# Rows of minus the row maxima in an attention kernel: split on VectorE as columns and turned by an ordinary product, in place of a transpose that is split after it

## The chip, the cores and the metric

The kernel runs on one core of a Trainium2 chip. The metric is the device time of one execution in microseconds (us); smaller is better. The time before is the median of three runs.

## The reference, cut to what matters

One transformer block with adaptive layer norm: softmax attention with 32 heads of width 16 over 2048 tokens of width 512, then a dense layer, Mish, and a dense layer (width 1792). What the change touches is the softmax:

```python
scores = jnp.einsum("bhqd,bhkd->bhqk", q, k) * scale
p = _softmax(scores, axis=-1)
o = jnp.einsum("bhqk,bhkd->bhqd", p, v)
```

A softmax subtracts from each row of scores (one query, one head) the largest score of that row before the exponential.

## The kernel before, in words

**Rounds and steps.** The work is cut into `NIT` = 32 rounds, one for each block of 512 queries and each group of four heads. A round has 16 steps; there are 512 steps after a prologue of `PRO` = 20. In every step TensorE makes, for the present round, four score products (L531, 128 keys by 512 queries, 64 rows of contraction each) that ScalarE turns into exponentials (L534), and the four products with V of two steps earlier (`pv`, L549). The maxima have to be known before the round begins, so in the same step TensorE also makes four products of a round that is one or two ahead (L482, 128 queries by 512 keys), of which VectorE takes the maxima (L484). The projections, the MLP and everything else are cut into pieces that stand beside these eight products (L135, on the other half of TensorE's rows). `step` writes the order of each engine by hand; an engine takes its instructions in that order.

**The ring.** The results of L482 and L531, and some others, go to `ring`, six banks of PSUM that are handed out in turn (`NRING` = 6). The ring gives a bank again after six others, so a product waits until the reader of the result six places earlier is done. In a step the order is maximum, score, maximum, score, maximum, score, score, maximum; below these are called m1 s1 m2 s2 m3 s3 s4 m4. So s4 waits for VectorE's reduction of m1 of the same step, and m4 for ScalarE's exponential of s1 of the same step.

**How the maxima get into the scores.** [...] The maxima come out of VectorE as columns (128 queries on the partitions), and are needed as rows.

**The functions that the change touches.** `neg_max(n)` is called at the end of the last maximum step of round n, t % 16 = 11 counted by steps, after that step's products. It reduces the four partial maxima of each query (`mx`, 128 x 64 values) to 16 values, twice (L505, v = 0 and 1), so that `mm` holds each maximum two times, 128 x 32. One step later, at the end of step t % 16 = 12 after `pv`, `max_rows(n, mm)` runs: TensorE transposes `mm` (L511) into a bank of the ring (32 x 128); ScalarE makes minus that, rounded to the short format, `mh` (L513); VectorE makes `mt` (L514): with the column `lows`, which is 0 for the high rows and -1 for the low rows, `mt` is `mh * lows - pt`, so minus the maximum in the high rows and the rounding's remainder in the low rows. In the step after that SyncE issues four DMAs (L520) that put `mt` into `qa`, where the scores of round n read it three steps later.

**Queues.** VectorE's queue in these steps holds the four reductions of each step and, between them, `neg_max` and the third instruction of `max_rows`; at some steps also a part of Mish (L732) or a reciprocal (L584). ScalarE's holds the exponentials, L513 and parts of Mish (L741 among them). GpSimd (POOL) does long element-wise work on 128 x 512 tiles in SBUF all along (L735 to L753, L95, L98, L820, L899).

Of the kernel before, what the change touches and what calls it, by code (L numbers as in the profile page):

```python
# [8 lines left out]
F32 = mybir.dt.float32  # L9
F32R = mybir.dt.float32r  # L10
AF = mybir.ActivationFunctionType
ALU = mybir.AluOpType
AX = mybir.AxisListType
# [5 lines left out]
def adaln_block(ctx: ExitStack, tc: tile.TileContext, x, wqkv, wo, w1, b1, w2, c, w_mod, out):  # L19
    nc = tc.nc  # L20
    P = 128
# [25 lines left out]
    out = out[0]  # L47
# [3 lines left out]
    cst = ctx.enter_context(tc.tile_pool(name="cst", bufs=1))  # L51
# [11 lines left out]
    ident = cst.tile([P, P], F32, name="ident")  # L63
# [10 lines left out]
    nc.gpsimd.memset(sel, 0.0)  # L74
    for k in range(DK):
        nc.gpsimd.memset(sel[32 * k:32 * k + 1, :], 1.0)
    lows = cst.tile([P, 1], F32, name="lows")
    nc.vector.tensor_reduce(out=lows[:32], in_=ident[:32, :32].rearrange("p (a v q) -> p v a q", a=4, v=2)[:, 1], op=ALU.add,
                            axis=AX.XY)
    nc.vector.tensor_scalar_mul(lows[:32], lows[:32], -1.0)  # L80
    modc = cst.tile([P, 4, DK], F32, name="modc")
    sil = cst.tile([P, DK], F32, name="sil")
    b1c = cst.tile([P, FT], F32, name="b1c")
# [66 lines left out]
    def ring(w=1):  # L150
        if w == 2 and ring_at[0] % 2:
            ring_at[0] += 1
        b = ring_at[0] % NRING
        ring_at[0] += w
        return ring_t[:, b, :] if w == 1 else ring_t[:, b:b + 2, :]
# [41 lines left out]
    def at(h, f):  # L197

        hooks.setdefault(h, []).append(f)
# [121 lines left out]
    with ExitStack() as es:  # L321
# [68 lines left out]
        for i in range(2):  # L390
            pr.append(ring())
            for k in range(DK):
                nc.tensor.matmul(pr[i][32 * k:32 * k + 32, :], sil[:, k:k + 1].to_broadcast([P, 32]), wma[i][:, k, :],
                                 start=True, stop=True)
# [68 lines left out]
    ap = ctx.enter_context(tc.tile_pool(name="ap", bufs=1, reuse_waits="tile"))  # L463
# [36 lines left out]
    def neg_max(n):  # L500

        mx = mxs.pop(n)
        mm = ap.tile([P, 4, 2, 4], F32, tag="mm", name="mm", bufs=2)
        for v in range(2):
            nc.vector.tensor_reduce(out=mm[:, :, v, :], in_=mx.rearrange("p s (j q) k -> p (s j) q k", j=2), op=ALU.max,  # L505
                                    axis=AX.X)
        ats.setdefault(16 * n + 16 - PRO, []).append(lambda: max_rows(n, mm))

    def max_rows(n, mm):
        pt = ring()  # L510
        nc.tensor.transpose(pt[:32, :P], mm.rearrange("p a v q -> p (a v q)"), ident)  # L511
        mh, mt = [ap.tile([32, P], F32R, tag=t, name=t, bufs=1) for t in ("mh", "mt")]
        nc.scalar.activation(mh, pt[:32, :P], AF.Identity, scale=-1.0)  # L513
        nc.vector.scalar_tensor_tensor(mt, mh.bitcast(F32), lows[:32], pt[:32, :P], op0=ALU.mult, op1=ALU.subtract)  # L514

        def put():
            for s in (1, 0):
                for j in range(2):
                    o = (2 * s + j) * 8
                    nc.sync.dma_start(  # L520
                        qa[(2 * n + j) % NR][64 * s + 48:64 * s + 50, :].rearrange("v (s q) -> v s q", s=4).bitcast(F32),
                        mt[o:o + 8, :].bitcast(F32))
        at(2 * (16 * n + 16 - PRO) + 2, put)
# [649 lines left out]
    def step(t):  # L1173
# [4 lines left out]
        if t < 0:  # L1178

            for i in range(2):  # L1180
                if tm < 16:
                    kb, jq = divmod(2 * tm + i, 8)
                else:
                    jq, kb = tm % 16 // 2, 2 * second + i
                max_pair(tm // 16, jq, kb)
            if second and tm % 16 == 15:
                neg_max(tm // 16)
            run_hooks(2 * t + 1)
            for f in ats.pop(t, []):
                f()  # L1190
            whole_units(2 * t + 1, CREDIT)
            do_specials(2 * t + 1)
            return
# [58 lines left out]
        if tm < T and tm % 16 == 15:  # L1252
            neg_max(tm // 16)
# [111 lines left out]
    t = T + 2  # L1365
# [32 lines left out]
```

## Time and profile before

| what | value |
|---|---|
| runs | 1705.08, 1706.13, 1705.99 us; median 1705.99 |
| span of the profiled execution | 1705.4 us; the page gives no time of that execution apart from its span |
| granted TensorE clock | 0.998 of full speed, mean over the span |
| busy: PE, PEld, DVE, ACT, POOL | 1678.7, 956.8, 1439.9, 1364.9, 808.0 us |
| L482, products for maxima | 1968, mean 427 ns |
| L484, their reductions | 1968, mean 682 ns |
| L534, exponentials | 2048, mean 601 ns |
| DMA | 240.08 MB, mean 141 GB/s |

How to read it: busy time counts overlapping instructions of one engine once; the end of a matmul is modelled, so a busy PE does not tell that TensorE could do no more. PEld is TensorE's loading of the stationary operand; its start is the better sign of when TensorE really turned to a product. An entry `[0.84 <-DVE mx L484]` in a timeline means that the engine stood idle 0.84 us and that the last semaphore it had waited for came from that instruction, which may have been given long before.

### The profile page before, as it was taken

The page shows a single profiled execution, that of the slowest core. Times are in us where ns is not written, and L with a number is a line of the kernel's source. Part 1 is how long each engine was busy: PE and PEld are TensorE (multiplying, and loading weights), DVE is VectorE, ACT ScalarE, POOL GpSimd, SP SyncE. Part 2 cuts the span into 40 slices and gives each one's busy share as a digit, 9 for nine tenths or more (in the row PEclk, how much of TensorE's full clock was granted, in tenths as well). Part 3 has the DMA queues.
Part 4 walks back from the last instruction along what each step waited for, and adds up shares of the span by engine and source line. Part 5 has one row for each costly group of instructions (what it writes and reads, how often), then busy time and mean ns, then how long its engine had stood idle before and what let it go on. Part 6 is the DMA issues. An engine that isn't in the chain of part 4 may idle for free.

```text
span 1705.4 us, 33628 instructions
## 1 busy us (share of the span) xinstructions
PE 1678.7 (98%) x12372; PEld 956.8 (56%) x12372; DVE 1439.9 (84%) x2368; ACT 1364.9 (80%) x2613; POOL 808.0 (47%) x829
## 2 busy tenths in 40 slices
PE   7999999999999999999999999999999999999999
PEld 5755655555445555555555555555555455554587
DVE  6888888888889998888889998888889988883377
ACT  6257777777778988888888988888888988888574
POOL 5155224665413464655423564555323655555442
PEclk9999999999999999999999999999999999999999
DMA  7677467777773342534355433424354433524261
GB/s 253 183 235 210 116 161 213 242 228 221 237 209 100 98 105 78 137 79 123 84 154 145 119 75 94 139 74 125 85 144 124 128 93 78 150 59 156 85 228 63
DMA packets 113997, 240.08 MB, mean 141 GB/s; under 512 B 24048, under 2 KB 49648, under 8 KB 107784
## 3 DMA queue, kind: packets, MB, share of 16 engines
q1 hardware_dynamic: 113832, 237.92, 48.8%
q8 instruction: 98, 1.61, 0.4%
q14 instruction: 67, 0.55, 0.1%
HBM read 179.95 MB, written 51.44 MB: 136 GB/s over the span
## 4 chain that ended last, share of the span: by engine, by line
PE 90%; DMA 4%; DVE 3%; ACT 1%; SPq 1%; issue 1%; POOL 0%; ACTq 0%; DVEq 0%; POOLq 0%
PE bk L549 28%; PE ring L482 21%; PE ring L531 19%; PE bk L135 12%; PE bk L129 3%; PE ring L1110 2%; PE ring L129 2%; DVE mx L484 1%; DMA qa<-mt 1%; DMA ka<-kscr 1%; DMA xt<-in_A_x 1%; PE ring L496 1%; ACT pr L534 1%; DMA w<-woscr 1%; DMA w<-w1scr 0%
## 5 line engine op out<-in xcount | busy, mean ns | idle before, releaser
L484 DVE TENSOR_REDUCE mx<-ring 128x1 f32<-128x512 f32 x1968 | 1222.1, 682 | 157.7 <-PE ring L482 134.1
L534 ACT ACTIVATE pr<-ring 128x512 f32<-128x512 f32 x2048 | 1085.6, 601 | 215.5 <-PE bk L135 131.2
L482 PE MATMUL ring<-ka,qa 64*128 64x512 f32 x1968 | 834.2, 427 | 5.2 <-DMA od<-ot 2.7
L531 PE MATMUL ring<-qa,ka 64*128 64x512 f32 x2048 | 724.5, 397 | 4.2 <-ACT pr L534 2.2
L482 PEld LDWEIGHTS ring<-ka,qa 64*128 64x128 f32 x1968 | 359.6, 184 | 405.8 <-DVE mx L484 341.2
L549 PE MATMUL bk<-pr,vg 128*32 128x512 f32 x4096 | 545.1, 604 | 0.0
L531 PEld LDWEIGHTS ring<-qa,ka 64*128 64x128 f32 x2048 | 373.8, 184 | 81.3 <-ACT pr L534 23.6
L135 PE MATMUL bk<-h,w 64*128 64x512 f32 (+1 forms) x1080 | 280.2, 393 | 0.1
L135 PE MATMUL bk<-w,a_h 64*128 64x512 f32 x632 | 213.0, 417 | 0.3 <-ACT pr L534 0.2
L135 PEld LDWEIGHTS bk<-h,w 64*128 64x128 f32 x1080 | 178.2, 184 | 12.3 <-ACT pr L534 3.7
L549 PEld LDWEIGHTS bk<-pr,vg 128*32 128x32 f32 x4096 | 80.7, 108 | 132.0 <-issue 124.6
L135 PE MATMUL bk<-w,a_l 64*128 64x512 f32 x316 | 124.0, 392 | 0.0
L135 PEld LDWEIGHTS bk<-w,a_h 64*128 64x128 f32 x632 | 104.7, 184 | 16.6 <-ACT pr L534 8.3
L899 POOL TENSOR_TENSOR y<-yd,y 128x512 f32<-128x512 f32 x44 | 56.8, 1292 | 89.5 <-ACT yd L898 84.4
L750 POOL TENSOR_TENSOR qq<-qq,rr 128x512 f32<-128x512 f32 x42 | 54.3, 1292 | 89.8 <-ACT rr L744 89.6
L734 POOL TENSOR_SCALAR qq<-ee 128x512 f32<-128x512 f32 x25 | 15.5, 619 | 168.0 <-ACT ee L728 168.0
L736 POOL TENSOR_TENSOR hb<-hb,ee 128x512 f32<-128x512 f32 x42 | 54.1, 1288 | 82.5 <-DVE ee L732 80.5
L135 PE MATMUL bk<-w,o_hl 64*128 64x512 f32 x288 | 79.6, 408 | 0.0
L98 POOL TENSOR_TENSOR a_l<-hb,a_h 128x512 fp32r<-128x512 f32 x53 | 72.0, 1359 | 4.4
L135 PEld LDWEIGHTS bk<-w,a_l 64*128 64x128 f32 x316 | 58.3, 184 | 3.9
L135 PE MATMUL bk<-h_h,wl 64*128 64x512 f32 x168 | 56.7, 418 | 0.0
L752 POOL TENSOR_TENSOR rr<-rr,qq 128x512 f32<-128x512 f32 x42 | 54.2, 1291 | 3.5
(189 smaller groups left out, 1844.2 us busy)
## 6 DMA issues: line engine op xcount, KB each, us to landing
ka<-kscr SPq DMA_DIRECT2D x124, 384.0 KB
w<-w2scr SPq DMA_DIRECT2D x56, 512.0 KB
w<-w1scr SPq DMA_DIRECT2D x46, 512.0 KB
vg<-vscr SPq DMA_DIRECT2D x32, 552.0 KB
qa<-qscr SPq DMA_DIRECT2D x124, 100.0 KB
kscr<-qh SPq DMA_DIRECT2D x16, 512.0 KB
qscr<-qh SPq DMA_DIRECT2D x32, 256.0 KB
hl<-in_B_w SPq DMA_DIRECT2D x28, 256.0 KB
```

The lines of the kernel that those rows point to most:

```text
L98: (nc.gpsimd if eng == "p" else nc.vector).tensor_sub(lo, src, hi.bitcast(F32))
L129: nc.tensor.matmul(acc, l, r, start=start, stop=stop)
L135: i = nc.tensor.matmul(acc, l[64 * g:64 * g + 64], r[64 * g:64 * g + 64], start=start and not g, stop=bool(stop and g))
L482: nc.tensor.matmul(pm, qt[64 * s:64 * s + 64, qs * P:(qs + 1) * P], kt[64 * s:64 * s + 64, kb * TB:(kb + 1) * TB], start=True, stop=True)
L484: nc.vector.tensor_reduce(out=mxs[n][:, s, 4 * j + qs, kb:kb + 1], in_=pm, op=ALU.max, axis=AX.X)
L531: nc.tensor.matmul(p_, kt[64 * s:64 * s + 64, kc * P:(kc + 1) * P], qt[64 * s:64 * s + 64, :], start=True, stop=True)
L534: e = nc.scalar.activation(pr, p_, AF.Exp, scale=SCALE)
L549: nc.tensor.matmul(accs[n][32 * h:32 * h + 32, :], vgs[n][:, o:o + 32], pts.pop((t, h)), start=(kc == 0), stop=(kc == 15))
L736: (nc.vector if tail else nc.gpsimd).tensor_mul(hb, hb, ee)
L750: nc.gpsimd.tensor_mul(qq, qq, rr)
L752: nc.gpsimd.tensor_mul(rr, rr, qq)
L899: nc.gpsimd.tensor_add(y[i], yd, y[i])
```

## The change

Minus the maximum and its split are made as columns, before the turn, and the turn is an ordinary product with an identity matrix that is kept in the short format. `neg_max` takes one reduction to a new tile `top` (one buffer), a multiplication by -1 that writes the high part rounded to the short format, and a `scalar_tensor_tensor` that takes the high part from minus `top` for the low part. `max_rows` multiplies `mm` with `identr`, and ScalarE copies the result to `mt`. `lows`, `mh` and VectorE's instruction on `mt` go. The DMAs, the steps in which things are issued and the ring's use stay.

```diff
-    lows = cst.tile([P, 1], F32, name="lows")
-    nc.vector.tensor_reduce(out=lows[:32], in_=ident[:32, :32].rearrange("p (a v q) -> p v a q", a=4, v=2)[:, 1], op=ALU.add,
-                            axis=AX.XY)
-    nc.vector.tensor_scalar_mul(lows[:32], lows[:32], -1.0)
+    identr = cst.tile([P, P], F32R, name="identr")
+    nc.vector.tensor_copy(identr, ident)
...
         mx = mxs.pop(n)
-        mm = ap.tile([P, 4, 2, 4], F32, tag="mm", name="mm", bufs=2)
-        for v in range(2):
-            nc.vector.tensor_reduce(out=mm[:, :, v, :], in_=mx.rearrange("p s (j q) k -> p (s j) q k", j=2), op=ALU.max,
-                                    axis=AX.X)
+        top = ap.tile([P, 4, 4], F32, tag="top", name="top", bufs=1)
+        mm = ap.tile([P, 4, 2, 4], F32R, tag="mm", name="mm", bufs=2)
+        nc.vector.tensor_reduce(out=top, in_=mx.rearrange("p s (j q) k -> p (s j) q k", j=2), op=ALU.max, axis=AX.X)
+        nc.vector.tensor_scalar_mul(mm[:, :, 0, :], top, -1.0)
+        nc.vector.scalar_tensor_tensor(mm[:, :, 1, :], top, -1.0, mm[:, :, 0, :].bitcast(F32), op0=ALU.mult,
+                                       op1=ALU.subtract)
         ats.setdefault(16 * n + 16 - PRO, []).append(lambda: max_rows(n, mm))
 
     def max_rows(n, mm):
         pt = ring()
-        nc.tensor.transpose(pt[:32, :P], mm.rearrange("p a v q -> p (a v q)"), ident)
-        mh, mt = [ap.tile([32, P], F32R, tag=t, name=t, bufs=1) for t in ("mh", "mt")]
-        nc.scalar.activation(mh, pt[:32, :P], AF.Identity, scale=-1.0)
-        nc.vector.scalar_tensor_tensor(mt, mh.bitcast(F32), lows[:32], pt[:32, :P], op0=ALU.mult, op1=ALU.subtract)
+        nc.tensor.matmul(pt[:32, :P], mm.rearrange("p a v q -> p (a v q)"), identr, start=True, stop=True)
+        mt = ap.tile([32, P], F32R, tag="mt", name="mt", bufs=1)
+        nc.scalar.copy(mt, pt[:32, :P])
```

## The prediction, made before the changed kernel was run

> **What bounds the kernel now.** I read the page first, then the timelines of two neighbouring steps, engine by engine.
>
> ```profile
> span 1705.4 us, 33628 instructions
> PE 1678.7 (98%) x12372; PEld 956.8 (56%) x12372; DVE 1439.9 (84%) x2368; ACT 1364.9 (80%) x2613; POOL 808.0 (47%) x829
> ```
>
> TensorE is nearly always busy, VectorE and ScalarE not far behind. Which of them ends a step is seen in the loads of TensorE's stationary operands. Below, one step with the transpose (661.03 to 664.18) and the next without (664.18 to 667.02):
>
> ```profile
> 661.03 0.16 PEld L549 LDWEIGHTS bk<-pr,vg 128*32 128x32 f32 x8 [0.25 <-issue]
> 662.03 0.10 PEld L511 LDWEIGHTS ring<-ident,mm 128*32 128x32 f32 x1 [0.84 <-DVE mx L484]
> 662.24 0.18 PEld L482 LDWEIGHTS ring<-ka,qa 64*128 64x128 f32 x1
> ...
> 663.64 0.18 PEld L531 LDWEIGHTS ring<-qa,ka 64*128 64x128 f32 x1 [0.17 <-DVE mx L484]
> 663.76 0.18 PEld L482 LDWEIGHTS ring<-ka,qa 64*128 64x128 f32 x1
> 664.18 0.16 PEld L549 LDWEIGHTS bk<-pr,vg 128*32 128x32 f32 x8 [0.24 <-issue]
> 665.18 0.18 PEld L482 LDWEIGHTS ring<-ka,qa 64*128 64x128 f32 x1 [0.84 <-DVE mx L484]
> ...
> 666.46 0.18 PEld L531 LDWEIGHTS ring<-qa,ka 64*128 64x128 f32 x1
> 666.60 0.18 PEld L482 LDWEIGHTS ring<-ka,qa 64*128 64x128 f32 x1
> 667.02 0.16 PEld L549 LDWEIGHTS bk<-pr,vg 128*32 128x32 f32 x8 [0.25 <-issue]
> ```
>
> The plain step lasts 667.02 - 664.18 = 2.84 us, the one with the transpose 3.15. The 0.84 us of idle time ahead of the first L482 are the products with V still running, not VectorE. Of the 0.31 us more, 662.24 - 662.03 = 0.21 are the transpose itself; the other 0.10 arise at the step's end.
>
> ```profile
> 659.38 0.35 DVE L505 TENSOR_REDUCE mm<-mx 128x16 f32<-128x64 f32 x2
> 659.71 2.48 DVE L484 TENSOR_REDUCE mx<-ring 128x1 f32<-128x512 f32 x4
> 662.65 0.33 DVE L514 SCALAR_TENSOR_TENSOR mt<-mh,lows,ring 32x128 fp32r<-32x128 f32 x1 [0.45 <-ACT mh L513]
> 662.91 2.47 DVE L484 TENSOR_REDUCE mx<-ring 128x1 f32<-128x512 f32 x4
> 665.71 2.48 DVE L484 TENSOR_REDUCE mx<-ring 128x1 f32<-128x512 f32 x4 [0.33 <-PE ring L482]
> ```
>
> VectorE's four reductions take 2.48 of the 2.84 us; it then idles about 0.35 us. But it is not free: the ring ties s4 to the reduction of m1. In the plain step that reduction starts at 665.71, 0.53 after the product's load, and lasts about 0.69 (to 666.40); s4's load follows at 666.46. A later start of the first reduction moves that load. The slack is read from the step with the transpose: there the first reduction starts at 662.91, 0.67 after the product's load instead of 0.53, s4's load follows it by 1.40 instead of 1.28, and yet the matmul keeps its pace:
>
> ```profile
> 663.51 0.40 PE L531 MATMUL ring<-qa,ka 64*128 64x512 f32 x1
> ...
> 663.74 0.39 PE L531 MATMUL ring<-qa,ka 64*128 64x512 f32 x1
> ```
>
> 0.23 us apart, about the pace of other products. So VectorE may be some 0.12 us late at the start of a step; what is over comes out of TensorE's time and is lost. The step's path is TensorE's, with VectorE and ScalarE tied within a tenth of a microsecond.
>
> **The change part by part.** It acts in 31 rounds (that of the first lies in the prologue).
>
> ```profile
> L505 DVE TENSOR_REDUCE mm<-mx 128x16 f32<-128x64 f32 x64 | 11.1, 215 | 1.1
> L514 DVE SCALAR_TENSOR_TENSOR mt<-mh,lows,ring 32x128 fp32r<-32x128 f32 x32 | 10.7, 333 | 15.9 <-ACT mh L513 15.9
> L511 PE MATMUL ring<-ident,mm 128*32 128x128 f32 x32 | 9.1, 284 | 0.0
> L513 ACT ACTIVATE mh<-ring 32x128 fp32r<-32x128 f32 x32 | 8.5, 266 | 11.0 <-PE ring L511 11.0
> L1110 PE MATMUL ring<-w,a_h 128*128 128x512 f32 x112 | 34.9, 393 | 0.0
> L129 PE MATMUL bk<-wl,h_h 128*128 128x256 f32 x48 | 8.2, 287 | 0.0
> ```
>
> *The turn.* Products in the short format take 393 ns for 512 columns and 287 ns for 256, so 106 ns for 256 columns; by that line 128 columns take 287 - 53 = 234, against 284 for the transpose: 0.05 us less in each round, -1.6 us in 31. No row has such a product with 128 columns. It can hardly take longer than one with 512 (393): +0.11 a round, +3.4 us. I take the line. [...]
>
> *VectorE's instruction on `mt` and its wait.* 0.33 us busy and 15.9 / 32 = 0.50 idle go in each round. In the step above this buys nothing: it made the first reduction 0.14 late, about the slack. What is late next is m4, which waits for s1's exponential. I count 0, at most the 0.10 at the step's end: -3.1 us.
>
> *ScalarE* keeps one small instruction (266 ns; the copy is of the same size). It takes over the waits for the last DMAs out of `mt`, while it idles 11.0 / 32 = 0.34 us for the turn anyway: 0. If that cover went, the exponentials behind it would be late by what is waited for. *The DMAs* into `qa` go out about 0.4 us earlier (no 0.33, no wait for `mh`), SyncE's queue frees as much earlier; no DMA is added. TensorE's matmuls waited for them 1.2 us in all:
>
> ```profile
> L531 PE MATMUL ring<-qa,ka 64*128 64x512 f32 x2048 | 724.5, 397 | 4.2 <-ACT pr L534 2.2 <-DMA qa<-mt 1.2 <-DVE mx L484 0.4
> ```
>
> 0 to -1.2 us; I take 0. The constants at the start are one small instruction instead of two, hidden by the first loads.
>
> *VectorE's columns.* The pair of reductions runs overlapped, 0.35 us from 659.38, and the next reduction followed at 659.71 without a gap: the pair just fills the idle time. Now there are three instructions, each reading what the one before wrote.
>
> ```profile
> 3.22 0.19 DVE L352 TENSOR_SCALAR sil_e<-sil_e 128x4 f32<-128x4 f32 x1 [1.57 <-ACT sil_e L351]
> 3.44 0.18 DVE L353 RECIPROCAL sil_e<-sil_e 128x4 f32<-128x4 f32 x1
> 3.66 0.16 DVE L354 TENSOR_TENSOR sil<-cc,sil_e 128x4 f32<-128x4 f32 x1
> ```
>
> Such a chain costs 0.16 to 0.19 each and 0.03 to 0.04 between (3.22 + 0.19 to 3.44). So 0.215 + 0.035 + 0.16 + 0.035 + 0.18 = 0.63 us instead of 0.35: the next reduction starts up to 0.28 later. 0.12 of that is slack, so between 0 (where the idle time is longer) and 0.16 us a round are lost. I take the middle, as no row says how the idle times lie: 31 x 0.08 = +2.5 us, bounds 0 and +5.0. `mm` is needed a step later, so its own lateness is hidden.
>
> *GpSimd in the way.* The last of the three, a `scalar_tensor_tensor`, reads two tensors in SBUF; the instruction on `mt` read one there and one in PSUM. An instruction with two SBUF inputs that meets a running GpSimd instruction is seen here:
>
> ```profile
> 599.37 1.74 DVE L732 SCALAR_TENSOR_TENSOR ee<-ee 128x512 f32<-128x512 f32 x1
> 601.04 3.07 DVE L484 TENSOR_REDUCE mx<-ring 128x1 f32<-128x512 f32 x5
> ```
> ```profile
> 599.27 1.29 POOL L753 TENSOR_TENSOR hb<-hb,rr 128x512 f32<-128x512 f32 x1
> ```
> ```profile
> L747 DVE SCALAR_TENSOR_TENSOR rr<-qq,rr 128x512 f32<-128x512 f32 x14 | 9.7, 692 | 0.5
> ```
> ```profile
> 599.80 0.16 PEld L549 LDWEIGHTS bk<-pr,vg 128*32 128x32 f32 x8 [0.24 <-issue]
> ...
> 602.96 0.18 PEld L531 LDWEIGHTS ring<-qa,ka 64*128 64x128 f32 x1 [0.41 <-DVE mx L484]
> ...
> 603.39 0.16 PEld L549 LDWEIGHTS bk<-pr,vg 128*32 128x32 f32 x8 [0.24 <-issue]
> ```
>
> It takes 1.74 us where 0.69 is usual: it ends 0.55, the time of its 512 elements, after GpSimd's instruction ends (599.27 + 1.29 = 600.56). TensorE's step there lasts 3.59 us instead of 2.84; s4's load waits for VectorE. So the wait is real and is paid. How often does GpSimd run where the new instruction will stand? I took the 31 stretches from 0.44 to 0.64 us after the first L505 (columns: length, then busy time of PE, PEld, DVE, ACT, POOL); the first, the last and the sum:
>
> ```profile
> 138.84:139.04 0.20, 0.20 (x4) 0.20 (x2) 0.20 (x1) 0.04 (x1) 0.12 (x2) 1.00 0.54 221
> ...
> 1548.21:1548.41 0.20, 0.20 (x6) 0.16 (x3) 0.00 (x0) 0.20 (x1) 0.20 (x1) 1.00 0.00 0
> sum 6.19, PE 5.97 PEld 5.25 DVE 5.59 ACT 2.17 POOL 3.50; mean PE 0.19 PEld 0.17 DVE 0.18 ACT 0.07 POOL 0.11
> ```
>
> GpSimd is busy in 3.50 of 6.19, 57%: some 17 of 31. With 1.29 us a GpSimd instruction, the mean rest is 0.64; less the slack and what the instruction would have taken, about 0.45. But only 13 rows show POOL busy for the whole 0.20; in two of them VectorE has no reduction waiting, and I leave out three more for instructions that end soon after. 8 x 0.45 = +3.6 us. Bounds: 0 (a 16-element instruction slips through) and 17 x 0.64 = +10.9.
>
> *Sum:* -1.6 + 0 + 0 + 2.5 + 3.6 = +4.5 us on the span of 1705.4, that is 1709.9. The span lies 0.6 below the median of the runs, 1705.99, so the forecast is 1710.5.
>
> **The rivals.** *The multiplication waits for GpSimd too.* It reads one SBUF tensor; no row shows such an instruction beside a running GpSimd. If it waits, it runs when GpSimd's instruction ends, and the `scalar_tensor_tensor` behind it meets the next GpSimd instruction, 0.09 us later (L753 ended 600.56; the next one is recorded at 600.65):
>
> ```profile
> 600.65 0.94 POOL L95 TENSOR_SCALAR a_h<-hb 128x512 fp32r<-128x512 f32 x1
> ```
>
> Each of the 8 places then costs 0.2 more, or, where the second wait is lost as well, about 1.3 more: 1712 to 1721; I set 1716. [...]
>
> *The chain hides and GpSimd does not matter:* -1.6 + 2.5 = +0.9, 1706.9.
>
> *VectorE's freed 0.83 us is what the step with the turn lacks.* The place is its end: if all 0.10 us come from the first reduction's 0.14 delay behind `mt`, they go in 31 rounds, -3.1; with the turn -4.7; and the chain must cost less than the 0.12 slack: 1701.3. For it: the wait of 0.17 us for VectorE ahead of the load at 663.64. Against: the matmul after it was on time, and the late one, m4 at 663.76, waits for ScalarE. It decides from the point where the longer chain stays within 0.12 us.
>
> [...]
>
> **How the numbers follow.** Forecast 1710.5: 0.42, its own range 1707 to 1714. Both wait: 0.20. Hidden: 0.18. Freed: 0.12. Slow product: 0.08. About 0.2%, 3.4 us, is what a measurement of this kernel can tell from no change. Faster by more (below 1702.6) is the freed case: 0.12. Within: the hidden one and 0.07 of the forecast's low end: 0.25. Slower (above 1709.4): 0.35 + 0.20 + 0.08 = 0.63. The range 1703 to 1721 leaves out most of the freed case and little above.
>
> **What would show it.** The load of L482 follows the turn's load by 0.16 us (0.21 now); by 0.3 if the product is slow. VectorE's `scalar_tensor_tensor` on `mm` has a median near 0.2 us and a maximum near 1 us; if its median too is long, or the multiplication's maximum is, the first rival holds. The steps that begin after `neg_max` grow (2.84 to 2.9, or 3.3 beside GpSimd); no VectorE idle time before `mt`. I am wrong if these steps stay at 2.84, or if the step with the turn falls from 3.15 by much more than 0.05.

## The result, and the profile after

| kernel | median of the runs, us | runs |
|---|---|---|
| before | 1706.06 | 6, 1705.08 to 1711.08 |
| after | 1718.14 | 6, 1715.0 to 1722.61 |

The ratio is 1.0063, with a 95% interval of 1.0044 to 1.0082: the changed kernel is slower, by some 10.7 us (0.0063 x 1706; 7.5 to 14.0 by the interval). The forecast was slower, 1710.5, a growth of 4.5 us. Direction and range held the result; the size was less than half of it.

The profiled execution took 1721.08 us with this span, 2.9 us over the median. The page:

```profile
span 1719.2 us, 33649 instructions
PE 1687.5 (98%) x12372; PEld 960.6 (56%) x12372; DVE 1444.8 (84%) x2367; ACT 1365.4 (79%) x2613; POOL 808.3 (47%) x829
```

VectorE's share of the span has not moved, 84%. The share cannot show what happened, because an instruction that waits inside the engine counts as busy: L504 below has 385 ns of busy time on average, up to 975, where its shortest takes 174. The same round as in the prediction, TensorE's loads of stationary operands in the step after `neg_max` (662.14 to 665.14) and in the step with the turn (665.14 to 668.25); L480 is the product for a maximum, L530 the score product, L548 the product with V. Before, the step after `neg_max` ran from 658.19 to the 661.03 that the prediction shows, 2.84 us; its first line, then the lines after:

```profile
658.19 0.16 PEld L549 LDWEIGHTS bk<-pr,vg 128*32 128x32 f32 x8 [0.25 <-issue]
```
```profile
662.14 0.16 PEld L548 LDWEIGHTS bk<-pr,vg 128*32 128x32 f32 x8 [0.24 <-issue]
663.13 0.18 PEld L480 LDWEIGHTS ring<-ka,qa 64*128 64x128 f32 x1 [0.84 <-DVE mx L482]
...
664.65 0.18 PEld L530 LDWEIGHTS ring<-qa,ka 64*128 64x128 f32 x1 [0.29 <-DVE mx L482]
664.72 0.18 PEld L480 LDWEIGHTS ring<-ka,qa 64*128 64x128 f32 x1
665.14 0.16 PEld L548 LDWEIGHTS bk<-pr,vg 128*32 128x32 f32 x8 [0.24 <-issue]
666.14 0.11 PEld L511 LDWEIGHTS ring<-identr,mm 128*32 128x32 f32 x1 [0.84 <-DVE mx L482]
666.32 0.18 PEld L480 LDWEIGHTS ring<-ka,qa 64*128 64x128 f32 x1
...
668.25 0.16 PEld L548 LDWEIGHTS bk<-pr,vg 128*32 128x32 f32 x8 [0.24 <-issue]
```

And VectorE in the same steps:

```profile
663.36 0.22 DVE L503 TENSOR_REDUCE top<-mx 128x16 f32<-128x64 f32 x1
663.61 0.17 DVE L504 TENSOR_SCALAR mm<-top 128x16 fp32r<-128x16 f32 x1
663.82 0.18 DVE L505 SCALAR_TENSOR_TENSOR mm<-top,mm 128x16 fp32r<-128x16 f32 x1
663.91 2.48 DVE L482 TENSOR_REDUCE mx<-ring 128x1 f32<-128x512 f32 x4
666.85 2.48 DVE L482 TENSOR_REDUCE mx<-ring 128x1 f32<-128x512 f32 x4 [0.46 <-PE bk L133]
```

In this round no GpSimd instruction holds the three up (one begins at 663.82, together with the third, which takes its usual 0.18). The step after `neg_max` lasts 3.00 us. Its first reduction starts 0.78 us after its product's load (663.91 - 663.13) and no longer 0.53. The last score product (s4) waits 0.29 us for it: the load of s4 is 1.52 us behind that of m1, where it was 1.28. The step with the turn lasts 3.11 us and not 3.15, although its first reduction is no longer late (666.85 is 0.53 after 666.32).

The small groups (columns: busy time, mean ns of one, idle time before and what ended it; `fp32r` is the short format, `F32R` in the code):

```profile
L504 DVE TENSOR_SCALAR mm<-top 128x16 fp32r<-128x16 f32 x32 | 12.3, 385 | 1.1
L513 ACT CAST mt<-ring 32x128 fp32r<-32x128 f32 x32 | 8.1, 254 | 15.9 <-PE ring L511 15.9
L511 PE MATMUL ring<-identr,mm 128*32 128x128 f32 x32 | 8.0, 249 | 0.3 <-DVE mm L505 0.3
L503 DVE TENSOR_REDUCE top<-mx 128x16 f32<-128x64 f32 x32 | 7.0, 220 | 1.1
L505 DVE SCALAR_TENSOR_TENSOR mm<-top,mm 128x16 fp32r<-128x16 f32 x32 | 6.6, 207 | 1.1
```

The same two VectorE lines with minimum, median and maximum of one instruction in ns:

```profile
L504 DVE TENSOR_SCALAR mm<-top x32: 174/210/975, 93.8 to 1560.9; 128x16 fp32r<-128x16 f32 x32
L505 DVE SCALAR_TENSOR_TENSOR mm<-top,mm x32: 174/176/1189, 94.1 to 1561.7; 128x16 fp32r<-128x16 f32 x32
```

The prediction expected the long durations on L505, the instruction with two inputs in SBUF. They are on L504, the multiplication, which has one: mean 385 ns, up to 975. It took 243 ns or more in 16 of its 32 rounds, and by GpSimd's timeline these are exactly the 16 in which a GpSimd instruction was running when it started; in the others it took 174 to 177. Round 17, VectorE and then GpSimd, whose only instruction in these 7 us this is:

```profile
895.27 0.22 DVE L503 TENSOR_REDUCE top<-mx 128x16 f32<-128x64 f32 x1
895.52 0.97 DVE L504 TENSOR_SCALAR mm<-top 128x16 fp32r<-128x16 f32 x1
896.53 0.17 DVE L505 SCALAR_TENSOR_TENSOR mm<-top,mm 128x16 fp32r<-128x16 f32 x1
896.62 2.48 DVE L482 TENSOR_REDUCE mx<-ring 128x1 f32<-128x512 f32 x4
```
```profile
895.17 1.29 POOL L819 TENSOR_TENSOR y<-yd,y 128x512 f32<-128x512 f32 x1 [4.45 <-ACT yd L818]
```
```profile
897.36 0.18 PEld L530 LDWEIGHTS ring<-qa,ka 64*128 64x128 f32 x1 [0.99 <-DVE mx L482]
```

GpSimd's instruction ends at 895.17 + 1.29 = 896.46, the multiplication at 895.52 + 0.97 = 896.49, and TensorE pays with 0.99 us of waiting ahead of s4. In round 27 the second wait is lost as well, to the next GpSimd instruction:

```profile
1371.34 0.40 DVE L504 TENSOR_SCALAR mm<-top 128x16 fp32r<-128x16 f32 x1
1371.77 1.19 DVE L505 SCALAR_TENSOR_TENSOR mm<-top,mm 128x16 fp32r<-128x16 f32 x1
```
```profile
1370.42 1.29 POOL L96 TENSOR_TENSOR a_l<-hb,a_h 128x512 fp32r<-128x512 f32 x1
1371.66 1.26 POOL L735 TENSOR_TENSOR hb<-hb,ee 128x512 f32<-128x512 f32 x1
```

L96 ends at 1371.71, the multiplication at 1371.74; L735 has begun by then, and L505 ends at 1372.96, 0.04 after L735 (1372.92). Behind these two waits TensorE's products stood still for 1.91 us, and then its granted clock fell to 0.50, from 1374.20 to 1377.61 by the trace's clock records. The eight products with V took 1.91 us there, against 1.06 in the same step before (columns of the last line: length, busy time of PE, PEld, DVE, ACT, POOL, granted clock, DMA share, GB/s):

```profile
1373.62 0.49 PE L530 MATMUL ring<-qa,ka 64*128 64x512 f32 x1 [1.91 <-DVE mx L482]
1374.11 1.91 PE L548 MATMUL bk<-pr,vg 128*32 128x512 f32 x8
```
```profile
1375.00:1376.00 1.00, 1.00 (x9) 0.05 (x1) 0.35 (x1) 0.00 (x0) 0.00 (x0) 0.50 0.00 0
```

The same columns are in e2 and e8 below, and there too the clock falls in this place after 1.91 us; in no other kernel does it.

**Where the time went.** To put the two traces side by side I took the time from the first load of one group of products with V to that of the next (the steps as above), after minus before, for each of the 511 steps. Rounds are counted by their `neg_max`, that in the prologue being 0. "Quiet" are 18 rounds; "beside GpSimd" ten (17, 19, 21, 23, 24, 25, 27 to 30) in which the multiplication took over 0.39 us. (In two of the quiet ones, 1 and 4, it took 0.30; they make 0.44 of the quiet sum.) Rounds 6 and 7 are left out of both: there that step moves between -1.2 and +2.2 us from kernel to kernel with a wait for a DMA, also in kernels whose columns are those of before. No maxima follow round 31.

| place | after - before, us |
|---|---|
| step after `neg_max`, 18 quiet rounds | +2.20 (0.12 each) |
| step after `neg_max`, 10 rounds beside GpSimd | +7.33 |
| step after that in round 27, at half the clock | +1.48 |
| step with the turn, 25 undisturbed rounds (all but 1, 6 to 9 and 27) | -0.037 each, -0.9 |
| wait for k and q near 490 us, two steps | +4.42 |
| prologue, tail | +0.66, +1.05 |
| all the rest | -2.4 |
| span (1719.2 - 1705.4) | +13.8 |

The first four rows, +10.1, are the size of the measured ratio. The wait near 490 us is taken up by an experiment.

### The profile page after: what moved, and what is told of

It is laid out like the page before. It is cut to its first block, busy times and chain, and to the rows that moved or that the text cites. A ratio compares the mean times of both kernels' runs of the same rounds, so it can differ in the third digit from the quotient of the medians.

```text
span 1719.2 us, 33649 instructions
## 1 busy us (share of the span) xinstructions
PE 1687.5 (98%) x12372; PEld 960.6 (56%) x12372; DVE 1444.8 (84%) x2367; ACT 1365.4 (79%) x2613; POOL 808.3 (47%) x829
## 4 chain that ended last, share of the span: by engine, by line
PE 89%; DVE 5%; DMA 3%; ACT 1%; issue 1%; SPq 0%; POOL 0%; ACTq 0%; DVEq 0%
PE bk L548 28%; PE ring L480 20%; PE ring L530 18%; PE bk L133 13%; PE bk L127 3%; DVE mx L482 3%; PE ring L1109 2%; PE ring L127 2%; ACT pr L533 1%; PE ring L494 1%; DMA qa<-qscr 1%; DMA ka<-kscr 0%; DMA w<-woscr 0%; DMA wma<-in_w_mod 0%; PE ring L842 0%
## 5 line engine op out<-in xcount | busy, mean ns | idle before, releaser
L480 PE MATMUL ring<-ka,qa 64*128 64x512 f32 x1968 | 837.4, 429 | 6.8 <-DMA od<-ot 4.4
L530 PE MATMUL ring<-qa,ka 64*128 64x512 f32 x2048 | 729.6, 398 | 7.8 <-DVE mx L482 5.1
L480 PEld LDWEIGHTS ring<-ka,qa 64*128 64x128 f32 x1968 | 360.6, 184 | 407.7 <-DVE mx L482 340.6
L548 PE MATMUL bk<-pr,vg 128*32 128x512 f32 x4096 | 546.8, 606 | 0.0
L530 PEld LDWEIGHTS ring<-qa,ka 64*128 64x128 f32 x2048 | 374.8, 185 | 87.4 <-DVE mx L482 27.8
L548 PEld LDWEIGHTS bk<-pr,vg 128*32 128x32 f32 x4096 | 80.8, 108 | 131.8 <-issue 124.4
L735 POOL TENSOR_TENSOR hb<-hb,ee 128x512 f32<-128x512 f32 x42 | 54.1, 1287 | 83.4 <-DVE ee L731 81.4
L96 POOL TENSOR_TENSOR a_l<-hb,a_h 128x512 fp32r<-128x512 f32 x53 | 72.0, 1358 | 4.4
```

What stands on the lines that cost most here:

```text
L96: (nc.gpsimd if eng == "p" else nc.vector).tensor_sub(lo, src, hi.bitcast(F32))
L480: nc.tensor.matmul(pm, qt[64 * s:64 * s + 64, qs * P:(qs + 1) * P], kt[64 * s:64 * s + 64, kb * TB:(kb + 1) * TB], start=True, stop=True)
L530: nc.tensor.matmul(p_, kt[64 * s:64 * s + 64, kc * P:(kc + 1) * P], qt[64 * s:64 * s + 64, :], start=True, stop=True)
L548: nc.tensor.matmul(accs[n][32 * h:32 * h + 32, :], vgs[n][:, o:o + 32], pts.pop((t, h)), start=(kc == 0), stop=(kc == 15))
L735: (nc.vector if tail else nc.gpsimd).tensor_mul(hb, hb, ee)
```

## The experiments

The kernels ran in three groups (e1, e2, e3, e5; e4, e6, e7, e8; e10 to e13), each on one chip beside the kernel before, whose medians in them are 1708.45, 1708.93 and 1708.42 us. "Quiet" and "beside" are the sums of the table above; "turn" is the mean change of the step with the turn in the same 25 rounds.

| kernel | median, us | ratio to before, 95% | quiet | beside | turn |
|---|---|---|---|---|---|
| after | 1718.14 | 1.0063 [1.0044, 1.0082] | +2.20 | +7.33 | -0.037 |
| e1_old_columns | 1705.78 | 0.9994 [0.9979, 1.001] | -0.05 | +0.03 | -0.038 |
| e2_old_turn | 1721.14 | 1.0081 [1.0052, 1.011] | +2.23 | +7.70 | +0.005 |
| e3_reductions | 1708.04 | 0.9998 [0.9984, 1.0012] | +0.91 | +0.50 | -0.038 |
| e5_two_input | 1711.49 | 1.0019 [1.0007, 1.0031] | +0.77 | +4.26 | -0.036 |
| e12_chain | 1710.58 | 1.0006 [0.9995, 1.0018] | +1.97 | +1.18 | -0.039 |
| e4_low_on_gpsimd | 1725.79 | 1.0101 [1.0085, 1.0116] | +0.03 | -0.07 | moved |
| e6_spread | 1713.86 | 1.0034 [1.0021, 1.0046] | +0.02 | +0.03 | moved |
| e10_mid | 1709.89 | 1.0009 [0.9995, 1.0022] | +0.01 | -0.02 | -0.038 |
| e13_before_put_later | 1713.89 | 1.0033 [1.002, 1.0047] | -0.05 | -0.02 | -0.001 |
| e7_before_later_loads | 1705.6 | 0.998 [0.997, 0.9991] | 0.00 | +0.03 | +0.001 |
| e8_after_later_loads | 1715.98 | 1.0041 [1.0028, 1.0053] | +2.16 | +7.51 | -0.037 |
| e11_mid_later_loads | 1707.77 | 0.9998 [0.9987, 1.001] | +0.05 | -0.03 | -0.039 |

**Half of the change alone.** e1 keeps the new turn and takes the columns back to two independent reductions; e2 keeps the new columns and takes back the transpose.

```diff
 e1
+        nc.vector.tensor_reduce(out=mm[:, :, 0, :], in_=src, op=ALU.max, axis=AX.X, negate=True)
+        nc.vector.tensor_reduce(out=top, in_=src, op=ALU.max, axis=AX.X, negate=True)
 e2
-        nc.tensor.matmul(pt[:32, :P], mm.rearrange("p a v q -> p (a v q)"), identr, start=True, stop=True)
+        nc.tensor.transpose(pt[:32, :P], mm.rearrange("p a v q -> p (a v q)").bitcast(F32), ident)
```

> The new turn and ScalarE's copy stay; VectorE's three dependent instructions in each round are replaced by two independent reductions as before (high part, and a second one into a tile that nobody reads). The low part is left out (zero). If the loss is VectorE's columns, the steps after neg_max return to 2.84 to 2.90 us, the step with the turn stays 0.04 shorter than before, and the time is 1 to 2 us under before, up to 4 over it where the long wait for loads near 490 us takes TensorE's clock down. If the loss came from the turn, the copy on ScalarE or the moved DMA waits, the time stays some 8 to 12 us over before.

> The new columns stay; only the product with the identity in the short format is a transpose again. If the turn is worth its 0.04 us a round, the step with the turn lasts 0.03 to 0.05 longer than in the changed kernel, 1.2 us over 31 rounds, and the time is 9 to 13 us over before. If the ordinary product were what costs, the time falls back to before.

The turn in e1 (min, median, max in ns) and in e2 (busy, mean):

```profile
L513 PE MATMUL ring<-identr,mm x32: 246/247/248, 94.3 to 1547.7; 128*32 128x128 f32 x32
```
```profile
L511 PE MATMUL ring<-ident,mm 128*32 128x128 f32 x32 | 9.2, 288 | 1.3 <-DVE mm L505 1.3
```

The halves come apart cleanly. The turn is worth 0.037 us in each round, which is the difference of the two durations (284 - 247), and nothing else of that step moved: VectorE's freed 0.83 us bought nothing. The columns are the whole of the loss.

**What in the columns costs.** e3 makes all three by reductions, the first two independent; e5 has the same two and the two-input instruction behind them; e12 has three reductions, each needing what the one before wrote, in the order of the changed kernel's instructions. Its second reads the 16 maxima from a half of `mm`, in four pieces of four; the multiplication read them from `top`, in one piece. In e1, e3 and e12 the low part is not computed and stays zero.

```diff
 e3
+        nc.vector.tensor_reduce(out=mm[:, 0, :, 0, :], in_=src, op=ALU.max, axis=AX.X, negate=True)
+        nc.vector.tensor_reduce(out=mm[:, 1, :, 0, :], in_=src, op=ALU.max, axis=AX.X)
+            nc.vector.tensor_reduce(out=mm[:, 0, :, 1, :], in_=mm[:, :, :, 0, :].rearrange("p w a q -> p a q w").bitcast(F32),
+                                    op=ALU.add, axis=AX.X, negate=True)
 e5
+        nc.vector.tensor_reduce(out=top, in_=src, op=ALU.max, axis=AX.X)
+        nc.vector.tensor_reduce(out=mm[:, :, 0, :], in_=src, op=ALU.max, axis=AX.X, negate=True)
         nc.vector.scalar_tensor_tensor(mm[:, :, 1, :], top, -1.0, mm[:, :, 0, :].bitcast(F32), op0=ALU.mult,
                                        op1=ALU.subtract)
 e12
+        nc.vector.tensor_reduce(out=mm[:, 1, :, 0, :], in_=src, op=ALU.max, axis=AX.X)
+        nc.vector.tensor_reduce(out=mm[:, 0, :, 0, :], in_=mm[:, 1, :, 0, :].unsqueeze(3).bitcast(F32), op=ALU.max, axis=AX.X,
+                                negate=True)
+            nc.vector.tensor_reduce(out=mm[:, 0, :, 1, :], in_=mm[:, :, :, 0, :].rearrange("p w a q -> p a q w").bitcast(F32),
+                                    op=ALU.add, axis=AX.X, negate=True)
```

> Three instructions in a chain stay, but all are reductions, which read one tensor: the two maxima (high part, and a second slab) and the sum of the two slabs, negated. Both slabs are rounded to the short format, so the low part is zero. If the loss has two parts, chain and waiting for GpSimd, the second goes: no instruction of the chain over 0.25 us, the steps after neg_max at about 2.95 to 3.0 in every round, and the time 4 to 6 us under the changed kernel, about 3 to 5 over before. If waiting for GpSimd is not it, the steps beside GpSimd (3.3 to 3.7 us in the changed kernel) stay as long and the time stays 8 to 12 over before.

> High part by a second reduction instead of the multiplication, low part by the scalar_tensor_tensor with two SBUF inputs: the case that the forecast took as the likeliest. If the two-input instruction waits for GpSimd by itself, its longest are near 0.8 to 1.0 us, in the rounds in which the multiplication was long in the changed kernel, and the time is 5 to 8 us over before, 2 to 3 under the changed kernel. If only the multiplication waits, all of them take 0.18 us and the time is 2 to 4 over before.

> The changed kernel with the two instructions behind the first reduction replaced by reductions that read and write the same places in the same order, each needing what the one before wrote (over one element, negated; and over the pair). Both parts are rounded to the short format, so the low part comes out zero: it is left out of what is computed. This holds the length of the chain apart from the waiting for GpSimd. Main theory: no instruction waits for GpSimd (0.17 to 0.22 us each in all rounds), the step after neg_max is 0.08 to 0.17 us longer in every round, quiet or not, +3 to +5 us in all; with the turn's -1.2, +2 to +4 us against before. Rival (the waiting alone costs, the chain is hidden): 0 to -1.5 us against before. Rival (any dependent instruction waits for GpSimd, whatever its form): as the changed kernel, +8 to +12 us.

Round 17 again, first in e12 (VectorE, then GpSimd), then in e5:

```profile
894.65 0.22 DVE L503 TENSOR_REDUCE mm<-mx 128x16 fp32r<-128x64 f32 x1
894.90 0.17 DVE L504 TENSOR_REDUCE mm<-mm 128x16 fp32r<-128x16 f32 x1
895.10 0.19 DVE L507 TENSOR_REDUCE mm<-mm 128x16 fp32r<-128x32 f32 x1
```
```profile
894.55 1.29 POOL L821 TENSOR_TENSOR y<-yd,y 128x512 f32<-128x512 f32 x1 [4.48 <-ACT yd L820]
```
```profile
890.02 0.21 DVE L505 TENSOR_REDUCE mm<-mx 128x16 fp32r<-128x64 f32 x1
890.26 0.85 DVE L506 SCALAR_TENSOR_TENSOR mm<-top,mm 128x16 fp32r<-128x16 f32 x1
```
```profile
889.79 1.29 POOL L820 TENSOR_TENSOR y<-yd,y 128x512 f32<-128x512 f32 x1 [4.46 <-ACT yd L819]
```

Beside the same GpSimd instruction, e12's second reduction reads 16 elements of SBUF and writes 16, as the multiplication did, and takes 0.17 us where the multiplication took 0.97; it and the third are done long before GpSimd ends (895.84). e5's two-input instruction waits: it ends at 891.11, GpSimd's at 891.08. That is no accident of round 17: in e12 a GpSimd instruction was running at the start of this reduction in 14 rounds, and it took 170 or 171 ns in every one. The input's layout is not the reason either, as the first reduction of the changed kernel reads `mx` in one piece and took 220 or 221 ns in all rounds, 14 of them beside GpSimd. So in these kernels the wait hangs on the kind of instruction (up to 975 ns for the multiplication, 966 for the two-input one, 171 for this reduction), not on its place or its data.

The sizes follow by subtraction. The chain alone (e12): 1.97 + 1.18 = +3.2 us. The waiting of the two-input instruction alone (e5 - e3): (0.77 + 4.26) - (0.91 + 0.50) = +3.6. In the changed kernel columns and waiting together cost 2.20 + 7.33 + 1.5 in round 27's second step, +11.0; less the chain, 7.9. Of these, 1.5 are the fall of the clock behind the two waits of round 27, and 6.4 the waiting itself, 2.8 more than e5 - e3. In round 17 the step grew by 0.87, against 0.67 in e5: the multiplication stands earlier in the queue, so it waits longer, and the third instruction comes out behind it. In round 27 it grew by 1.52 against 0.28, as there the third waits as well. e12's ratio alone, 1.0006, would not tell its chain from nothing; its steps do. For e3 and e5 my expected sums, 3 to 5 and 5 to 8 over before, were too high.

**Other ways to get the columns.** e4 leaves the low part to GpSimd. e6 has four one-input reductions, two in this step and two in the next. Both move the turn and the DMAs into `qa` one step later.

```diff
 e4
+        nc.vector.tensor_reduce(out=mm[:, :, 0, :], in_=src, op=ALU.max, axis=AX.X, negate=True)
+        nc.vector.tensor_reduce(out=top, in_=src, op=ALU.max, axis=AX.X, negate=True)
+        nc.gpsimd.tensor_sub(mm[:, :, 1, :], top, mm[:, :, 0, :].bitcast(F32))
 e6
+        nc.vector.tensor_reduce(out=pr[:, 0], in_=src, op=ALU.max, axis=AX.X)
+        nc.vector.tensor_reduce(out=pr[:, 1].bitcast(F32R), in_=src, op=ALU.max, axis=AX.X, negate=True)
+        def split():
+            nc.vector.tensor_reduce(out=mm[:, :, 0, :], in_=src, op=ALU.max, axis=AX.X, negate=True)
+                nc.vector.tensor_reduce(out=mm[:, :, 1, :], in_=pr.rearrange("p w a q -> p a q w"), op=ALU.add,
+                                        axis=AX.X, negate=True)
+        ats.setdefault(16 * n + 16 - PRO, []).append(split)
 both
-        ats.setdefault(16 * n + 16 - PRO, []).append(lambda: max_rows(n, mm))
+        ats.setdefault(16 * n + 17 - PRO, []).append(lambda: max_rows(n, mm))
-        at(2 * (16 * n + 16 - PRO) + 2, put)
+        at(2 * (16 * n + 17 - PRO) + 2, put)
```

> The changed kernel with minus the maximum written by one reduction, the maximum by a second that does not wait for it, and the difference of the two taken by GpSimd; the turn and the DMAs one step later. VectorE then has two independent one-input reductions, as before the change, and no instruction with two inputs in SBUF. Main theory (the loss is VectorE's chain and its waiting for GpSimd): the step after neg_max returns to the length of before (0 to +1 us in all), the turn keeps its 0.04 us a round, so 0 to 2 us under the kernel before, ratio 0.999 to 1.000. Rival (one small subtraction more on GpSimd or the later DMAs cost TensorE something): 2 us or more over before, seen as a wait of the score product for qa. A rival of the main theory that puts the loss on the three instructions as such (their number): the loss stays away here as well, so this run cannot hold it apart from the chain; e6 can.

> The changed kernel with VectorE's work as four small reductions, two at the end of the step t%16 = 11 (the maximum, and minus the maximum rounded), two one step later (minus the maximum rounded again, into mm, and minus the sum of the first pair, the low part); the turn and the DMAs one step later than in the changed kernel. One input each and no multiplication. Main theory: no reduction waits for GpSimd (all of them 0.18 to 0.23 us), the step after neg_max as before, the next one up to 0.1 longer where VectorE has no slack, the turn 0.04 shorter: -1.5 to +2 us against before. Rival (VectorE's number of small instructions counts, two more than before a round, about 0.2 us each): +4 to +8 us.

In both the step after `neg_max` is as before, as the theory has it. Both are slower all the same, and my expected times were wrong. The later DMAs stood among e4's rivals alone; the turn's wait for GpSimd stood nowhere. In e4 the turn waited for GpSimd in three rounds, 2.2 to 2.9 us each, 7.8 us by its matmul; GpSimd's own timeline in one of these rounds shows why. In e6 the score product waited 8.0 us for the DMAs into `qa`, where before had 1.2. First e4, its turn and its timeline, then e6:

```profile
L511 PE MATMUL ring<-identr,mm 128*32 128x128 f32 x32 | 8.1, 254 | 7.8 <-POOL mm L506 7.8
```
```profile
432.08 1.31 POOL L663 TENSOR_TENSOR hl<-hl,gate 128x512 f32<-128x512 f32 x1 [3.58 <-DMA hl<-in_B_w]
...
437.34 0.22 POOL L506 TENSOR_TENSOR mm<-top,mm 128x16 fp32r<-128x16 f32 x1
```
```profile
L536 PE MATMUL ring<-qa,ka 64*128 64x512 f32 x2048 | 726.1, 397 | 11.1 <-DMA qa<-mt 8.0 <-ACT pr L539 2.1 <-DVE mx L482 0.6
```

e4's subtraction itself takes 0.22 us, but it stands in GpSimd's queue behind an instruction that waited 3.58 us for a DMA, and runs 7.9 us after VectorE's second reduction ended (429.43). e13 moves the DMAs alone, in the kernel before. e10 has e6's four reductions, the second pair in the middle of the next step, and leaves the turn and the DMAs where the changed kernel has them (the lines against e6).

```diff
 e13
-        at(2 * (16 * n + 16 - PRO) + 2, put)
+        at(2 * (16 * n + 17 - PRO) + 2, put)
 e10
-        ats.setdefault(16 * n + 16 - PRO, []).append(split)
-        ats.setdefault(16 * n + 17 - PRO, []).append(lambda: max_rows(n, mm))
+        at(2 * (16 * n + 16 - PRO) + 1, split)
+        ats.setdefault(16 * n + 16 - PRO, []).append(lambda: max_rows(n, mm))
-        at(2 * (16 * n + 17 - PRO) + 2, put)
+        at(2 * (16 * n + 16 - PRO) + 2, put)
```

> The kernel before with one thing moved: the four DMAs that put mt into qa are issued one step (2.8 us) later. Theory from e6 (the DMAs of these rounds land just in time where they stand): waits of the score product for qa in the rounds with weight loads, 6 to 12 us in all, in the steps t%16 that read the first rows. Rival (e6 and e4 lost that time for their own reasons, the turn's place in the ring among them): within 2 us of before.

> The four small reductions of e6 (two at the end of the step t%16 = 11, two in the middle of the next), with the turn and the DMAs where the changed kernel has them. e6 lost 9.6 us in the steps two and three after its turn, waiting for the DMAs into qa that went out a step later than in the changed kernel, and nothing in the step after neg_max. Main theory: without that move the loss goes; the step after neg_max as before (0 to +0.5 us in all), the step with the turn 0.04 us shorter or, if the middle reductions are late for it, up to 0.1 longer: -3 to +2 us against before, ratio 0.998 to 1.001, 8 to 12 us under the changed kernel. Rival (two small reductions in the middle of a step cost as much as they last, 0.38 us, because VectorE has no slack there): +6 to +12 us.

e13:

```profile
L531 PE MATMUL ring<-qa,ka 64*128 64x512 f32 x2048 | 726.2, 398 | 15.9 <-DMA qa<-mt 13.0 <-ACT pr L534 2.2 <-DVE mx L484 0.4
```

One step later is too late: the wait for `qa` grows from 1.2 to 13.0 us in this execution (1720.51 us, the longest of its 12), nearly all of it in four rounds (3.7, 1.4, 1.2 and 7.8 us in the step that reads the rows first), and the median by 5.5. e10, without that move, has no loss in the step after `neg_max`, the turn's gain whole, and no cost of the two reductions in the middle of a step. Its ratio is 1.0009 where e6 has 1.0034, so it mends what the change lost, yet it is not faster than before. Its prologue is 3.42 us longer than that of before (0.74 in e1): the hook in the middle of a step lies behind both maxima there, and the one turn in the prologue waits 2.90 us:

```profile
97.15 0.11 PEld L517 LDWEIGHTS ring<-identr,mm 128*32 128x32 f32 x1 [2.90 <-DVE mm L510]
```

That is a flaw of this experiment. Without it, some 2.7 us less (3.42 - 0.74) are to be expected; it was not run.

**The wait near 490 us.** In the first block of rounds TensorE waits there for k and q of a later round. e7 and e8 send six weight loads of the MLP later, so that they do not stand in the queue ahead of k and q; e11 does so with e10.

```diff
-            more_w2(h + 1, NA)
+            more_w2(h + 1, DK)
+            at(h + 16, lambda: more_w2(h + 17, NA - DK))
...
-            load(h + 9, w1s, load_w1, range(2))
+            load(h + 20, w1s, load_w1, range(2))
```

> The kernel before with 4 of the weight loads of the MLP's second layer and the two of its first layer issued 11 to 16 half steps later in the first block, so that they do not stand in the queue ahead of the k and q of the round at 490 us. Theory: TensorE's wait for that DMA, 3.6 us in the profiled execution of before, falls under 1 us, and the time by about 3 us (ratio 0.998). Rival (the wait is not set by these loads): the wait stays and the time is within 1 us, or the loads are late in their turn and the time is 1 to 5 us over.

> The changed kernel with the same loads later. In the profiled execution of the changed kernel TensorE waited 5.3 us for k and q at 490 us and its granted clock then fell to 0.50 for about 5 us; in that of before it waited 3.6 us and the clock stayed at 1.00. If this wait is a part of the 12 us between the two that is not of the change itself: the wait and the fall of the clock go, and the time is 4 to 8 us under the changed kernel's (1710 to 1714). VectorE's part remains: 8 to 11 us over the kernel before with the same loads later. Rival (the columns cause the wait): it comes back here, or at another load.

> e10 with the later weight loads of e7, which gave a ratio of 0.998 to the kernel before. If the two gains add: 2 to 4 us under e10, 4 to 6 under the kernel before (ratio 0.997). If the wait at 490 us and the place of the DMAs into qa depend on one another, as the same queues carry both: no gain over e10.

The changed kernel around 490 us (length, busy time of PE, PEld, DVE, ACT, POOL, granted clock, DMA share, GB/s), then e7:

```profile
490.00:495.00 5.00, 0.72 (x4) 0.69 (x6) 0.00 (x0) 0.28 (x1) 1.12 (x1) 0.86 0.58 120
495.00:500.00 5.00, 5.00 (x24) 2.34 (x22) 2.93 (x5) 2.28 (x4) 0.00 (x0) 0.50 0.02 3
```
```profile
490.00:495.00 5.00, 5.00 (x44) 2.85 (x40) 4.54 (x8) 4.38 (x9) 1.29 (x1) 1.00 0.59 184
```

With the loads later the wait is gone in e7, e8 and e11 (that step is 2.8 us shorter than in before) and the clock stays at 1.00. e7 is faster than the kernel before, and is the only one of these that is by its interval. The columns do not cause this wait: e8 has no wait and still loses 2.16 + 7.51 in its columns, and its ratio over e7's is 1.0041 / 0.998 = 1.0061, the 1.0063 of the change itself. The wait's length moves from kernel to kernel with the same loads (from -2.3 in e3 to +3.7 in e2, against before). It is also gone in e4, e6 and e13 (-2.8), which leave these loads where they were; there TensorE had already lost 3.9 to 9.0 us three and four steps earlier, with the wait for `qa`. So the loads are one way to be rid of it, not the only one. e8 was expected at 1710 to 1714 and came out at 1716, in a group whose kernel before ran 2.9 us above its first runs (1708.93, 1706.06). e11 gains 2.1 us over e10, by medians with overlapping ranges; the 4 to 6 us under the kernel before that were expected of the two gains together did not come (0.65 by medians, ratio 0.9998).

## Why the prediction was right in direction and short in size

- *The turn*, -1.6 forecast: 247 ns (e1; the mean of 249 in the changed kernel has in it the 0.32 us of round 27, at half the clock), not the 234 of the line through 512 and 256 columns; the step gives 0.037 a round, -1.2 in 31. Right. The slow product (chance 0.08) did not come: the transpose takes 284 ns, the product 247, where the upper bound was the 393 of 512 columns. No run shows a turn for which the product is slower.
- *VectorE's instruction on `mt` and its wait*, counted at nothing: right. The first reduction of that step came 0.14 us earlier, the step shrank by the turn alone. The rival of the freed 0.83 us falls: e1, which frees the same and pays nothing for columns, has the same -0.038.
- *ScalarE and the DMAs*, 0: ScalarE's instruction took 254 ns against 266. No instruction of TensorE waited for `mt` in the changed kernel; but in other kernels with equally early DMAs the waits were as long as before (1.6 us in e1, 1.2 before, of the score product's matmuls), so no gain is shown.
- *The longer chain*, +2.5 (0 to +5.0): e12 gives +3.2. The slack of about 0.12 us was read about rightly: in the round shown the first reduction came 0.25 us later and the step grew by 0.16, so 0.09 was free.
- *GpSimd in the way*, +3.6 on the `scalar_tensor_tensor`: as a price of that instruction it was right, as e5 - e3 gives +3.6, though in part by luck. The mean rest of 0.64, less the slack of 0.12 and the instruction's own 0.18, is 0.34 and not the 0.45 that the sum took; and e5's instruction waited in 13 of 32 rounds (0.24 us or more), not in 8, some of them at next to no cost for the step (rounds 21 and 23). **The step that failed** is the one ahead of it: the prediction let only "the last of the three" wait. The multiplication waits too, in 16 of 32 rounds by the trace (0.24 us or more, where 0.174 is its shortest), earlier in the queue and so for longer. With it the waiting comes to 6.4 us instead of 3.6, and to 7.9 with the fall of the clock in round 27, for which the prediction had no term.
- *The rival that did hold* is the first, "the multiplication waits for GpSimd too", in each part: 0.2 us more at a place (0.87 against 0.67), and once, in round 27, the second wait lost as well. Its 1716 and its range, 1712 to 1721, fit the measured 1718.14; the half clock in round 27 and the wait near 490 us were not in it. With a chance of 0.20 it stood too low beside a row-less assumption that one input means no wait. That one input can be enough, the prediction had no row for. The runs show it for the multiplication (up to 975 ns for 16 elements in SBUF) and show no wait of a reduction over 16 such elements (171 at most). Why the two differ no run shows.

What stays open: why the wait near 490 us is longer in some kernels than in others with the same loads.

## What to carry to other kernels

A small VectorE instruction was not priced by its elements here. With two tensors read in SBUF (e5: 174 ns at least, up to 966), or as an element-wise one with one (a multiplication by a constant: 174 at least, up to 975), it waited for the rest of the GpSimd instruction that ran at that moment, and the engine's busy share did not show it (84% before and after). So look at the maximum of its duration, and for a small step choose a form that does not wait (here a reduction, even over one element: 171 ns at most). And work that is moved off a tight queue by "only one step" takes its DMAs with it: one step later cost 5.5 us here by itself (e13, medians), half of what the change had lost.

## What the runs showed of the hardware that was not expected

- A one-input multiplication, SBUF to SBUF, of 128 x 16 values took 0.174 us at least with no GpSimd instruction running at its start and up to 0.975 beside one, and ended 0.03 us after that one (896.49 and 896.46 in round 17); e12's TENSOR_REDUCE with input and output in SBUF waited in none of its 32 rounds (min, median, max):

```profile
L504 DVE TENSOR_REDUCE mm<-mm x32: 170/170/171, 93.8 to 1553.1; 128x16 fp32r<-128x16 f32 x32
```

- The product in the short format with 128 columns takes 247 ns (median in the changed kernel and in e1), the transpose of the tile of the same size 284 (median in the kernel before and in e2).
- The granted clock after an idle stretch of TensorE's products was not a matter of its length alone. It fell to 0.50 after 1.91 us in round 27 of the changed kernel, and 3.7 us into the 4.42 us near 490 us. In the kernel before it kept 1.00 after 2.75 us (0.35 + 1 + 1 + 0.40):

```profile
490.00:491.00 1.00, 0.65 (x8) 0.00 (x0) 0.70 (x2) 1.00 (x3) 0.36 (x1) 1.00 1.12 160
...
493.00:494.00 1.00, 0.60 (x6) 0.62 (x8) 0.10 (x1) 0.00 (x0) 0.00 (x0) 1.00 0.64 180
```

  e10 and e11 idle for the same 2.47 us in the prologue, ahead of the same product (from 94.68 and from 94.14); e10 keeps 1.00, e11 falls to 0.50. One microsecond of each behind it, e10 first:

```profile
98.00:99.00 1.00, 1.00 (x6) 0.73 (x4) 0.00 (x0) 0.00 (x0) 0.65 (x1) 1.00 0.67 260
```
```profile
98.00:99.00 1.00, 1.00 (x4) 0.70 (x3) 0.00 (x0) 0.00 (x0) 0.53 (x1) 0.50 0.69 268
```

  So the same 2.47 us ended in a fall once and once not, and 1.91 us in a fall where 2.75 did not. What decides it no run shows; the lengths rest on the modelled ends of the matmuls, which may hide some of the idle time.
